# Weight conversion ordered behind head pairs, and three streamed operands moved to another place in SBUF

## The chip, the cores and the metric

One core of a Trainium2 chip runs the whole program. The metric is the device time of one execution in microseconds (us), and the median of several executions is compared. The engines are TensorE (PE, with its weight loads, PEld, shown apart), VectorE (DVE), ScalarE (ACT), GpSimd (POOL) and the DMA queue that SyncE (SP) issues.

## The reference, cut to what matters

```python
def phi(x):
    proj = x @ w_phi
    proj = proj - max(abs(proj), axis=-1)
    return concatenate([exp(proj), exp(-proj)], axis=-1)
q_p, k_p = phi(q), phi(k)                  # 8 batches x 8 heads, 576 x 64 -> 576 x 256
num = q_p @ (k_p.T @ v)
den = q_p @ sum(k_p, axis=sequence) + 1e-6
x   = num / den                            # heads side by side: 8 x 576 x 512
u   = x + (relu(x.T @ w_tok1) @ w_tok2).T  # 576 -> 256 -> 576
out = u + relu(u @ w_ch1) @ w_ch2          # 512 -> 1536 -> 512
```

Everything is float32. `w_ch1` and `w_ch2` are `wc1` and `wc2` in the kernel. They come from the host as 8-byte numbers.

## The kernel before, in words

Heads are worked in 32 pairs, four to a batch. Five generators emit the program, and `weave` (L547) decides by a virtual clock whose step comes next. Each generator yields the cost of its step, which is divided by its share: `keys` and `queries` 5.2, `token_stream` 8.0, `load_weights` 10.0, `channel_stream` 19.5. A generator that yields None waits in the emission for another one. The order so emitted is a priority: a scheduler then fixes each engine's own order by times that it models, and may let a later instruction whose operands are ready go first. On the chip each engine keeps the order that came out.

`keys` (L246) loads a pair, makes feature maps of the keys in five groups (`less_max`, L184: a product with the feature weights, the absolute maximum, a subtraction; then two exponentials, L265), and `add_kv` (L276) sums features times values in PSUM: `pkv`, L287, with `kp` stationary and the value tile `v` streamed. When the fifth group is in, ACT copies the sum to SBUF (`kv`, L298). `queries` (L304) does the same for queries, turns the feature rows with TensorE transposes (`pt`, L343, the identity `ident` streamed), takes exponentials and multiplies by `kv` (`pn`). Pairs 0 to 3 (`PLAIN`) are multiplied in plain float32, with `wp` streamed (L209) and `qf` streamed (L377). Later pairs are split into two float32r parts and take three products (`mm3`, L70) with `wp2`, `qh` and `ql` streamed. For pairs 0 to 7 (`EARLY`) the reciprocal of the denominator goes through DRAM in small DMAs on SP's queue (L391 to L399).

`token_mix` (L416) needs two attended pairs of a batch. It transposes with `ident` streamed (`px`, L423). `channel_mix` (L462) takes 256 tokens at a time through six up-projections (`h`, stationary `wc1_h` and `wc1_l`, streamed `uh` and `ul`) and six down-projections (`acc`, stationary `wc2`, streamed `gh` and `gl`), 24 matmuls of 256 columns each. An up-projection `ep` waits in the emission until `wc2` rows 2ep and 2ep+1 are converted (L504).

`load_weights` (L137) converts the weights from 8-byte numbers to two float32r parts. One `convert` (L107) is a DMA of 512 KB on SP (`rawc`, L118), an absolute value on ACT (L124), four bit operations on DVE (L125 to L128, tile `bitsc`), a rounding copy on ACT and a subtraction on POOL. After seven small conversions for `w1` and `w2` there are 24 large ones, in three groups of eight: four of 512 columns of `wc1` and four row blocks of `wc2`. Four staging buffers (`late0` to `late3`) are shared by them. `pace()` yields 8.0 before pair 3 is attended and 1.0 after.

SBUF pools lie one behind the other: `cst`, `wk`, `st`, `odd`. `cst` begins with a tile of 32 bytes, `st` with one of 192 bytes, and nearly every other tile of `cst`, `wk` and `st` is a multiple of 512 bytes. So stationary operands (in `cst` and `wk`) share one starting phase modulo 512 bytes, and the float32r streamed operands (in `st`) share one that lies 192 bytes further. `ident` and `wp` are in `cst`. The value tiles `v0` and `v1` are in `odd`, with 65 floats (260 bytes) from one slice to the next.

Of the kernel before, what the change touches and what calls it, by code (L numbers as in the profile page):

```python
# [8 lines left out]
F32 = mybir.dt.float32  # L9
# [3 lines left out]
AF = mybir.ActivationFunctionType  # L13
# [4 lines left out]
P = 128  # L18
B, H, S, D = 8, 8, 576, 64
NP = H // 2  # L20
F = 128
# [4 lines left out]
PLAIN = 4  # L26
EARLY = 8
BORROWED = 18
STAGES = 4
LAST = 15  # L30
LAG = 0.02
# [11 lines left out]
def mixer_kernel(ctx, tc, qk, vm, vt, w_phi, w1, w2, wc1, wc2d, out):  # L43
    nc = tc.nc

    cst = ctx.enter_context(tc.tile_pool(name="cst", bufs=1))
# [3 lines left out]
    st = ctx.enter_context(tc.tile_pool(name="st", bufs=2))  # L50
    odd = ctx.enter_context(tc.tile_pool(name="odd", bufs=2))
# [10 lines left out]
    def split(hi, lo, raw, eng_hi, eng_lo):  # L62

        if eng_hi is nc.scalar:
            nc.scalar.copy(hi, raw)
        else:
            eng_hi.tensor_copy(hi, raw)
        eng_lo.tensor_tensor(lo, raw, hi.bitcast(F32), op=ALU.subtract)
# [6 lines left out]
                             skip_group_check=group_ok)  # L75


    ident = cst.tile([P, P], F32, name="ident")
    make_identity(nc, ident)
    eps = odd.tile([P, 1], F32, tag="eps", name="eps", bufs=1)  # L80
    nc.gpsimd.memset(eps, 1e-6)
    wp2 = st.tile([P, 2, F], F32R, tag="wp2", name="wp2", bufs=1)
    wp = cst.tile([P, F], F32, name="wp")
    nc.scalar.dma_start(wp[D:], w_phi)
    nc.scalar.dma_start(wp[:D], w_phi)
    split(wp2[:, 0], wp2[:, 1], wp, nc.vector, nc.vector)
# [8 lines left out]

    vtiles = []
    for j in range(2):
        t = odd.tile([P, 5, 2, D + 1], F32, tag=f"v{j}", name=f"v{j}", bufs=1)
        nc.gpsimd.memset(t[:, 4], 0.0)
        nc.gpsimd.memset(t[:, 0:4, :, D:], 1.0)  # L100
        for i in range(2):
            nc.gpsimd.memset(t[i * D:(i + 1) * D, 4, i, D:], 1.0)
        vtiles.append(t)

    nstage = [0]

    def convert(hi, lo, srcs, name, tag=None):  # L107

        w, n = hi.shape
        if tag is None:  # L110
            tag = f"late{nstage[0] % STAGES}"
            nstage[0] += 1
        raw = wk.tile([P, 4, 256], U32, tag=tag, name=f"raw{name}", bufs=3 if tag == "xt1" else 1)
        raw = raw.rearrange("p a b -> p (a b)")[:w, :2 * n]
        at = 0
        for src in srcs:
            m = src.shape[1]
            nc.sync.dma_start(raw[:, 2 * at:2 * (at + m)].bitcast(I64), src)  # L118
            at += m
        raw = raw.rearrange("p (n two) -> p n two", two=2)  # L120
        top, low = raw[:, :, 1], raw[:, :, 0]
        m = wk.tile([P, 512], U32, tag="bits", name=f"bits{name}", bufs=3)[:w, :n]

        nc.scalar.activation(m.bitcast(F32), top.bitcast(F32), AF.Abs)  # L124
        nc.vector.tensor_scalar(m.bitcast(F32), m.bitcast(F32), LEAST, MOST, op0=ALU.max, op1=ALU.min)  # L125
        nc.vector.tensor_scalar(m, m, 3, 0x3FFFFFF8, op0=ALU.logical_shift_left, op1=ALU.bitwise_and)
        nc.vector.scalar_tensor_tensor(m, top, 0xC0000000, m, op0=ALU.bitwise_and, op1=ALU.bitwise_or)
        nc.vector.scalar_tensor_tensor(m, low, 29, m, op0=ALU.logical_shift_right, op1=ALU.bitwise_or)  # L128
        split(hi, lo, m.bitcast(F32), nc.scalar, nc.gpsimd)

    def flat(t):
        return t.rearrange("p a b -> p (a b)")

    def pace():
        return 1.0 if NP - 1 in attended else 8.0

    def load_weights():  # L137
        for u in (0, 3):
            s = UNITS[u][2]
            convert(flat(w1_h[:, u:u + 2]), flat(w1_l[:, u:u + 2]),  # L140
                    [w1[s + o:s + o + P] for o in (0, P)], f"1_{u}")
            yield 1.0
        convert(w1_h[:D, 2], w1_l[:D, 2], [w1[512:]], "1_2")
        for w in (w1_h, w1_l):
            nc.scalar.copy(w[D:, 2], w[:D, 2].bitcast(F32))
        yield 0.4
        for u in range(NT):
            rows = w2[u * P:(u + 1) * P]
            convert(w2_h[:, u, :256], w2_l[:, u, :256], [rows[:, :256]], f"2_{u}")
            yield 0.5  # L150
            convert(w2_h[:, u, 256:], w2_l[:, u, 256:], [rows[:, 512:], rows[:, 256:512]], f"3_{u}")
            yield 0.7
        for e in range(0, E, 512):
            for c in range(NC_):
                convert(wc1_h[:, c, e:e + 512], wc1_l[:, c, e:e + 512],
                        [wc1[c * P:(c + 1) * P, e:e + 512]], f"c1_{c}_{e}")
                yield pace()
            for k in range(e // P, e // P + 4):
                src = wc2d[k * P:(k + 1) * P]
                late = k - (NE - STAGES)  # L160
                if late < 0:
                    t, tag = cst.tile([P, 2, C], F32R, name=f"wc2_{k}"), None
                else:
                    t = wk.tile([P, 2, C], F32R, tag=f"late{late}", name=f"wc2_{k}", bufs=1)
                    tag = f"late{late + 1}" if late + 1 < STAGES else "xt1"
                wc2.append(t)
                convert(t[:, 0], t[:, 1], [src], f"c2_{k}", tag)
                loaded.add(k)
                yield pace()

# [13 lines left out]
    def less_max(ts, units, name, base=None):  # L184
# [4 lines left out]
        if base == D:  # L189
            ps = ps_a.tile([P, 2, 2, F], F32, tag=f"a{nplain['k'] % 2}", name=f"pp{name}")  # L190
            nplain["k"] += 1
        elif base == 0 and (nplain["q"] % 2 == 0 or nplain["q"] >= BORROWED):
            ps = ps_h.tile([P, 2, 2, F], F32, tag="h", name=f"pp{name}")
# [52 lines left out]
    def keys():  # L246
        groups = [[(0, 0), (0, 1)], [(0, 2), (0, 3)], [(1, 0), (1, 1)], [(1, 2), (1, 3)], [None]]
        todo = None
        for i in range(B * NP):
            yield from until(lambda: i < 2 or i - 2 in asked)  # L250
            if i < PLAIN:
                load_plain(i)
            else:
                load(i)
            v_sb, queue = vtiles[i % 2], nc.sync if i else nc.scalar
            queue.dma_start(v_sb[:, 0:4].rearrange("p u j d -> p (u j) d")[:, :, :D], vm[i])
            for j in range(2):
                queue.dma_start(v_sb[j * D:(j + 1) * D, 4, j, :D], vt[i, j])
            plain = D if i < PLAIN else None
            ts = pairs[i] if i < PLAIN else stack(raws[i], D, f"k{i}")  # L260
            for g, us in enumerate(groups):
                pm = less_max(ts, us, f"k{i}_{g}", plain)
                kp = wk.tile([P, 2, 2, F], F32, tag="kp", name=f"kp{i}_{g}")
                for sg in range(2):
                    nc.scalar.activation(kp[:, :len(us), sg], pm[:, :len(us)], AF.Exp, scale=1.0 - 2.0 * sg)  # L265
                yield 0.22
                if todo:
                    add_kv(*todo)
                    yield 0.82
                todo = (i, g, us, kp, v_sb)  # L270
        add_kv(*todo)
        yield 0.82
# [3 lines left out]
    def add_kv(i, g, us, kp, v_sb):  # L276
        if g == 0:
            pkvs[0] = ps_k.tile([P, 2, 2, D + 1], F32, tag="kv", name=f"pkv{i}")
        pkv = pkvs[0]
        for n, u in enumerate(us):  # L280
            for sg in range(2):
                if u is None:
                    o = pkv[:, sg].rearrange("p j d -> p (j d)")
                    v = v_sb[:, 4].rearrange("p j d -> p (j d)")
                else:
                    o, v = pkv[:, sg, u[0]], v_sb[:, u[1], u[0]]
                nc.tensor.matmul(o, kp[:, n, sg], v, start=g == 0 and n == 0 and sg == 0, stop=u is None,  # L287
                                 skip_group_check=True)
        if g < 4:
            return  # L290

        both = []
        for k in range(1 if i < PLAIN else 2):
            kv = wk.tile([P, 2, 4, D], F32 if i < PLAIN else F32R, tag=f"kv{k}", name=f"kv{k}_{i}", bufs=1)
            for at, src in ((slice(0, 4, 3), pkv[:, :, :, :D]),
                            (slice(1, 3), pkv[:, :, :, D:].to_broadcast([P, 2, 2, D]))):
                if k == 0:
                    nc.scalar.copy(kv[:, :, at], src)  # L298
                else:
                    nc.vector.tensor_tensor(kv[:, :, at], src, both[0][:, :, at].bitcast(F32), op=ALU.subtract)  # L300
            both.append(kv)
        kvs[i] = both
# [103 lines left out]
    def until(cond):  # L406
        while not cond():
            yield None
# [138 lines left out]
    def weave(streams):  # L547
# [3 lines left out]
        while streams:  # L551
# [13 lines left out]

    weave([(keys(), 5.2, True), (queries(), 5.2, True), (token_stream(), 8.0, False),
           (load_weights(), 10.0, False), (channel_stream(), 19.5, False)])


# [40 lines left out]
```

## Time and profile before

| | us |
|---|---|
| median of 3 executions | 1162.64 |
| range of the 3 | 1160.67 to 1170.23 |
| the profiled execution, device time | 1164.33 |
| its span, first to last instruction | 1162.2 |
| PE / PEld busy in the span | 1121.3 / 1090.5 |
| DVE / ACT / POOL busy in the span | 685.7 / 659.4 / 570.1 |

The profile is one execution. "Busy" counts the time in which an engine had an instruction in work. Matmuls overlap one another in the record, so the time from one matmul to the next is read from the chain of waits (a piece with its count), and not from the mean length of one. In the windows, "x" is the number of instructions that touch the stretch, and PEclk is the mean granted TensorE clock in it, 1.00 for 2.4 GHz and 0.50 for 1.2 GHz.

### The profile page before, as it was taken

To read this page: it belongs to the slowest core of one execution; us is meant where nothing else is said; L and a number is where in the kernel's file an instruction comes from. 1 tells how busy PE (TensorE), PEld (TensorE's weight loads), DVE (VectorE), ACT (ScalarE), POOL (GpSimd) and SP (SyncE) were. 2 spreads that over 40 slices of the span, in tenths; PEclk is the share of its full clock that TensorE was granted. 3 is DMA by queue.
4 is the path that set the end of the run, shared out by engine and by line. 5 is a ranking of instruction groups with operands and counts; after the bars stand their busy time and mean duration, and the time that the engine had idled before them with its cause. 6 is when DMAs were issued, how large, how long until landed. Compare 5 with 4: busy or idle time off the path is not lost.

```text
span 1162.2 us, 24135 instructions
## 1 busy us (share of the span) xinstructions
PE 1121.3 (96%) x9032; PEld 1090.5 (94%) x9032; DVE 685.7 (59%) x1446; ACT 659.4 (57%) x1845; POOL 570.1 (49%) x734
## 2 busy tenths in 40 slices
PE   8987799999999999999999999999999999999998
PEld 7766699998999899999999999999999989999998
DVE  7989763536656665667566465573666666553111
ACT  5678785666656665666657465563655666441110
POOL 3347773555545564566646354563554655430000
PEclk9988999999999999999999999999999999999999
DMA  8564130111111011111111011110111110000000
GB/s 224 162 187 135 42 88 24 47 43 54 32 28 52 21 41 41 32 49 32 32 49 33 19 32 50 32 50 13 38 48 33 50 31 11 20 1 19 19 19 19
DMA packets 72531, 56.77 MB, mean 49 GB/s; under 512 B 49920, under 2 KB 63648, under 8 KB 72416
## 3 DMA queue, kind: packets, MB, share of 16 engines
q1 hardware_dynamic: 71056, 54.89, 16.7%
q8 instruction: 71, 1.16, 0.4%
q10 hardware_dynamic: 1360, 0.36, 0.2%
q14 instruction: 44, 0.36, 0.1%
HBM read 45.72 MB, written 9.51 MB: 48 GB/s over the span
## 4 chain that ended last, share of the span: by engine, by line
PE 85%; ACT 5%; DVE 4%; DMA 3%; issue 1%; POOL 1%; SPq 0%; POOLq 0%; DVEq 0%; ACTq 0%
PE acc L74 25%; PE h L74 25%; PE pkv L287 9%; PE pn L74 7%; PE ph L74 4%; PE pa L74 3%; PE pt L343 3%; PE ppk L205 2%; PE ppq L205 2%; DMA inv<-few 1%; PE px L423 1%; PE pn L377 1%; PE ppk L209 1%; ACT qh L356 1%; ACT qf L350 1%
## 5 line engine op out<-in xcount | busy, mean ns | idle before, releaser
L74 PE MATMUL acc<-gh,wc 128*128 128x256 f32 x1728 | 336.5, 282 | 0.2 <-ACT gh L489 0.2
L74 PEld LDWEIGHTS acc<-gh,wc 128*128 128x128 f32 x1728 | 274.0, 189 | 0.5 <-ACT gh L489 0.4
L74 PE MATMUL h<-ul,wc_h 128*128 128x256 f32 x864 | 243.4, 282 | 1.9 <-POOL ul L470 1.8
L74 PE MATMUL h<-uh,wc_h 128*128 128x256 f32 x864 | 244.8, 284 | 0.5 <-DVE gl L490 0.5
L74 PE MATMUL h<-uh,wc_l 128*128 128x256 f32 x864 | 243.7, 282 | 0.0
L74 PE MATMUL acc<-gl,wc 128*128 128x256 f32 x864 | 242.3, 282 | 0.0
L287 PE MATMUL pkv<-v,kp 128*128 128x65 f32 (+1 forms) x1152 | 165.7, 280 | 0.4 <-ACT kp L265 0.3
L74 PEld LDWEIGHTS h<-ul,wc_h 128*128 128x128 f32 x864 | 163.1, 189 | 2.7 <-POOL ul L470 2.7
L74 PEld LDWEIGHTS h<-uh,wc_h 128*128 128x128 f32 x864 | 162.6, 188 | 1.2 <-DVE gl L490 1.1
L74 PEld LDWEIGHTS h<-uh,wc_l 128*128 128x128 f32 x864 | 163.4, 189 | 0.0
L74 PEld LDWEIGHTS acc<-gl,wc 128*128 128x128 f32 x864 | 162.8, 188 | 0.0
L287 PEld LDWEIGHTS pkv<-v,kp 128*128 128x128 f32 x1152 | 156.9, 203 | 4.0 <-issue 1.8
L265 ACT ACTIVATE kp<-pmk 128x256 f32<-128x256 f32 (+1 forms) x320 | 109.3, 392 | 89.0 <-POOL pmk L221 83.7
L357 POOL TENSOR_TENSOR ql<-qf,qh 128x320 fp32r<-128x320 f32 (+1 forms) x112 | 92.8, 828 | 135.9 <-ACT qh L356 133.2
L490 DVE SCALAR_TENSOR_TENSOR gl<-h,gh 128x512 fp32r<-128x512 f32 x108 | 74.0, 686 | 140.3 <-ACT gh L489 139.6
L350 ACT ACTIVATE qf<-pt 128x320 f32<-128x320 f32 (+1 forms) x256 | 105.2, 414 | 84.6 <-PE pt L343 83.9
L489 ACT ACTIVATE gh<-h 128x512 fp32r<-128x512 f32 x108 | 64.6, 598 | 102.5 <-PE h L74 101.8
L74 PE MATMUL pn<-qh,kv 128*128 128x320 f32 (+1 forms) x448 | 114.9, 297 | 1.7 <-DVE pq L214 0.8
L402 POOL TENSOR_TENSOR xt<-xt,den 128x320 f32<-128x320 f32 x64 | 53.8, 840 | 116.7 <-DVE den L401 36.6
L357 DVE TENSOR_TENSOR ql<-qf,qh 128x320 fp32r<-128x320 f32 (+1 forms) x112 | 71.1, 635 | 65.0 <-ACT qh L356 64.6
L221 POOL TENSOR_TENSOR pmk<-pk,mxk 128x256 f32<-128x256 f32 (+1 forms) x140 | 86.8, 620 | 30.0 <-DVE mxk L219 23.2
L180 POOL TENSOR_TENSOR stq<-raw,stq 64x512 fp32r<-64x512 f32 (+1 forms) x56 | 79.8, 1424 | 40.5 <-ACT stq L179 36.4
(109 smaller groups left out, 2420.8 us busy)
## 6 DMA issues: line engine op xcount, KB each, us to landing
raw<-in_qk SPq DMA_DIRECT2D x27, 576.0 KB, 4.0
rawc<-in_wc SPq DMA_DIRECT2D x24, 512.0 KB, 4.8
v<-in_vm SPq DMA_DIRECT2D x31, 256.0 KB, 3.9
out_x<-xt SPq DMA_DIRECT2D x12, 256.0 KB, 2.2
out_x<-xt SPq DMA_DIRECT2D x16, 192.0 KB, 2.0
raw<-in_w SPq DMA_DIRECT2D x8, 256.0 KB, 3.5
out_x<-xt SPq DMA_DIRECT2D x16, 128.0 KB, 3.0
pair<-in_qk SPq DMA_DIRECT2D x8, 160.0 KB, 3.8
```

The source lines that it names most:

```text
L74: nc.tensor.matmul(o, a, m, start=first and i == 0, stop=last and i == 2, skip_group_check=group_ok)
L180: nc.gpsimd.tensor_tensor(t[lo:lo + D], src, t[base:base + D].bitcast(F32), op=ALU.subtract)
L205: nc.tensor.matmul(ps[:, i].rearrange("p two f -> p (two f)"), t[:, c:c + P], wp2.rearrange("p two f -> p (two f)"), start=True, stop=True)
L221: eng.tensor_tensor(pm[:, :n], pr, mx[:, :n].unsqueeze(2).to_broadcast([P, n, F]), op=ALU.subtract)
L265: nc.scalar.activation(kp[:, :len(us), sg], pm[:, :len(us)], AF.Exp, scale=1.0 - 2.0 * sg)
L287: nc.tensor.matmul(o, kp[:, n, sg], v, start=g == 0 and n == 0 and sg == 0, stop=u is None, skip_group_check=True)
L343: nc.tensor.transpose(ptr[:, n], r, ident)
L350: nc.scalar.activation(full, src, AF.Exp, scale=1.0 - 2.0 * sg)
L357: (nc.gpsimd if sg else nc.vector).tensor_tensor(lo, full, hi.bitcast(F32), op=ALU.subtract)
L402: nc.gpsimd.tensor_tensor(x, x, den, op=ALU.mult)
L489: nc.scalar.activation(gh, ph, AF.Relu)
L490: nc.vector.scalar_tensor_tensor(gl, ph, 0.0, gh.bitcast(F32), op0=ALU.max, op1=ALU.subtract)
```

## The change

The 24 large conversions get a gate for each group of eight. In the emission, group 0, 1 and 2 wait until the `kv` copy of pair 2, 3 and 4 has been emitted, and the first ACT instruction of each conversion is put behind that copy in ACT's queue (`issue_after` adds an order on the same engine and no semaphore). The identity, the plain feature weights and the value tiles move into the pool `st`, the value slices with 128 floats (512 bytes) from one to the next, so that all of them begin at the phase of the other streamed operands. The two value tiles grow from 2,600 to 5,120 bytes a partition each. The product of the fifth key group writes and reads its two heads as a strided shape in place of a flat one.

```diff
+FROM = 2
...
-    ident = cst.tile([P, P], F32, name="ident")
+    ident = st.tile([P, P], F32, tag="ident", name="ident", bufs=1)
...
-    wp = cst.tile([P, F], F32, name="wp")
+    wp = st.tile([P, F], F32, tag="wp", name="wp", bufs=1)
...
-        t = odd.tile([P, 5, 2, D + 1], F32, tag=f"v{j}", name=f"v{j}", bufs=1)
+        t = st.tile([P, 5, 2, 128], F32, tag=f"v{j}", name=f"v{j}", bufs=1)[:, :, :, :D + 1]
...
-    def convert(hi, lo, srcs, name, tag=None):
+    summed = {}
+
+    def convert(hi, lo, srcs, name, tag=None, behind=None):
...
-        nc.scalar.activation(m.bitcast(F32), top.bitcast(F32), AF.Abs)
+        with tc.issue_after(summed[behind].ins) if behind is not None else nullcontext():
+            nc.scalar.activation(m.bitcast(F32), top.bitcast(F32), AF.Abs)
...
         for e in range(0, E, 512):
+            pair = FROM + e // 512
+            yield from until(lambda: pair in summed)
             for c in range(NC_):
                 convert(wc1_h[:, c, e:e + 512], wc1_l[:, c, e:e + 512],
-                        [wc1[c * P:(c + 1) * P, e:e + 512]], f"c1_{c}_{e}")
+                        [wc1[c * P:(c + 1) * P, e:e + 512]], f"c1_{c}_{e}", None, pair)
                 yield pace()
...
-                convert(t[:, 0], t[:, 1], [src], f"c2_{k}", tag)
+                convert(t[:, 0], t[:, 1], [src], f"c2_{k}", tag, pair)
...
-                    o = pkv[:, sg].rearrange("p j d -> p (j d)")
-                    v = v_sb[:, 4].rearrange("p j d -> p (j d)")
+                    o, v = pkv[:, sg], v_sb[:, 4]
...
-                    nc.scalar.copy(kv[:, :, at], src)
+                    summed[i] = nc.scalar.copy(kv[:, :, at], src)
```

## Rows read from the trace of the kernel before

**Rows 1.** The page: PE's busy time, then its tenths and granted clock in 40 slices.
```profile
PE 1121.3 (96%) x9032; PEld 1090.5 (94%) x9032; DVE 685.7 (59%) x1446; ACT 659.4 (57%) x1845; POOL 570.1 (49%) x734
...
PE   8987799999999999999999999999999999999998
...
PEclk9988999999999999999999999999999999999999
```

**Rows 2.** Windows: stretch, length, PE, PEld, DVE, ACT, POOL busy (count), PEclk, DMA share, GB/s.
```profile
27.00:58.00 31.00, 30.70 (x109) 24.47 (x107) 30.04 (x61) 21.01 (x49) 11.43 (x8) 1.00 0.58 172
58.00:73.00 15.00, 13.34 (x88) 10.41 (x87) 12.42 (x29) 13.14 (x34) 8.48 (x7) 1.00 0.68 205
73.00:100.00 27.00, 19.48 (x91) 15.74 (x92) 25.02 (x45) 18.56 (x45) 12.96 (x11) 0.81 0.63 164
100.00:130.00 30.00, 25.51 (x153) 21.61 (x152) 27.33 (x56) 24.60 (x64) 23.20 (x22) 0.89 0.34 97
130.00:160.00 30.00, 26.34 (x206) 24.75 (x205) 20.05 (x47) 25.00 (x70) 20.73 (x27) 1.00 0.21 59
...
150.00:200.00 50.00, 49.88 (x427) 49.48 (x426) 23.36 (x56) 33.66 (x95) 28.83 (x40) 1.00 0.15 43
```

**Rows 3.** Chain of waits, two pieces of one kind: start, length, what, count.
```profile
37.74 3.60 PE pkv L287 x16
...
63.17 1.73 PE pkv L287 x16
```

**Rows 4.** ACT in order of time: the kv copies of pairs 2, 3 and 4.
```profile
72.97 0.65 ACT L298 COPY kv<-pkv 128x256 f32<-128x256 f32 x2
...
100.62 0.64 ACT L298 COPY kv<-pkv 128x256 f32<-128x256 f32 x2
...
127.49 0.64 ACT L298 CAST kv<-pkv 128x256 fp32r<-128x256 f32 x2
```

**Rows 5.** Windows, instructions on bitsc alone: DVE, ACT, POOL busy (count), PEclk, DMA.
```profile
27.00:58.00 31.00, 22.96 (x33) 9.80 (x16) 9.42 (x6) 1.00 0.58 172
58.00:73.00 15.00, 7.73 (x13) 4.00 (x7) 5.68 (x4) 1.00 0.68 205
73.00:100.00 27.00, 20.88 (x27) 8.93 (x14) 8.99 (x7) 0.81 0.63 164
100.00:130.00 30.00, 17.95 (x21) 6.21 (x10) 8.05 (x6) 0.89 0.34 97
```

**Rows 6.** Chain of waits between 80 and 110 us, three of its pieces.
```profile
80.49 6.51 DMA inv<-few
...
100.13 1.79 DMA inv<-few
...
109.37 1.42 DVE bitsc L128
```

**Rows 7.** Chain of waits, pieces of matmuls after the start of the channel mix.
```profile
155.02 2.83 PE h L74 x24
...
163.85 0.79 PE h L74 x7
...
182.58 2.13 PE h L74 x18
...
303.11 1.59 PE h L74 x14
...
306.97 0.22 PE pt L343 x2
...
307.30 0.59 PE acc L74 x5
...
1050.38 0.57 PE pa L74 x5
...
1053.67 0.61 ACT ah L448
...
1152.59 5.67 PE acc L74 x48
```

## The prediction

> **What bounds the kernel now.** I read the page first, then windows over the first 200 us, then the chain of waits, and last the rows of the weight conversion. The page shows PE busy for 96% of the span, and the slices place nearly all that is missing in the first five of forty, some 145 us [rows 1]. From 150 us on PE has no room: 49.88 of 50 us busy, while DVE is at 23.36 [rows 2]. So a change can gain only in two ways: less time lost before about 155 us, or a faster pace of the matmuls after it. The two halves of the change aim at one each.
>
> The start has two parts. Up to 58 us PE is busy without a break (30.70 of 31 us), though DVE is nearly full beside it (30.04) [rows 2]. The pace there is low: sixteen products of features and values take 3.60 us at 37.74 and 1.73 us at 63.17 [rows 3]. The window's 1.00 can't be right for that stretch: the pace is half, which fits the lower level of 1.2 GHz and then 2.4 GHz. From 58 to 160 us PE is idle for 1.66, 7.52, 4.49 and 3.66 us of the four stretches, 17.3 us in all, and the granted clock averages 0.81 and 0.89 in the middle two [rows 2]. There DVE is the fuller engine (25.02 of 27, 27.33 of 30), and the chain runs through conversion work on DVE and the small transfers of the denominators [rows 2, 6].
>
> **The conversions, step by step.** A large conversion is four DVE instructions. Before 73 us 33 + 13 of them were touched, so 46/4 = 11.5 conversions, and pair 2's copy, behind which the first group now stands, comes at 72.97 [rows 4, 5]. Those 11.5 must be done later.
>
> (a) 27 to 58 us: 22.96 us of DVE, 9.80 of ACT and 9.42 of POOL leave [rows 5]. PE loses nothing there today, so I cost this at 0. The bound on the gain is PE's 0.30 us of idle; a loss has no source, since PE's work there doesn't change. Its cover is gone, though: DVE time that was free beside a slow PE is given up.
>
> (b) 58 to 73 us: 7.73 us of DVE leave [rows 5]. PE's idle 1.66 us there can go, and pairs 2 and 3 reach their copies sooner. What follows is the stretch with the lower clock: at a mean of 0.81 over 27 us the lower level held for 27 x 0.19 x 2 = 10.3 us; at PE's busy share there (19.48/27 = 0.72) half of 7.4 us is lost, 3.7 us. Bounds of (b): 0 to -5.4 us, and +3.7 if the lower level comes once more. I take -4, as pair 2's chain loses most of its bit operations.
>
> (c) From 73 us on: 11.5 more conversions. One costs 4 x 20.88/27 = 3.1 us of DVE at 73 to 100 and 4 x 17.95/21 = 3.4 us at 100 to 130, against 4 x 22.96/33 = 2.8 us in the early stretch [rows 5]: where POOL is busier the same four instructions take longer. So 11.5 x 3.2 = 37 us of DVE enter. The room is 87 - 72.40 = 14.6 us up to 160 [rows 2]; 22 us are left over. They need not be done by then. The first up-projection that reads the third group of `wc1` is the fifth, whose piece starts at 182.58 [rows 7], and the third group may start after pair 4's copy, now at 127.49 [rows 4]. From 150 to 200 us DVE has 26.6 us of room [rows 2], so the rest fits if DVE takes conversions behind the attention's work. No semaphore is added: the absolute values are only ordered behind the copy on ACT, so nothing on ACT waits longer than the copy. Queued behind a late conversion are: on ACT its rounding copy and then the exponentials of the next keys, on POOL its subtraction and then those of the features, and on SP its 512 KB load (24 in all, one each) ahead of the loads of `raw` and `v` and the denominators' small transfers. One of these took 6.51 us where another took 1.79 [rows 6]; one more such delay is 4.7 us, on the chain only until pair 3 is attended. Bounds of (c): 0, and +22 if the 22 us of DVE all end on the path. I take +2, near the lower end, because of the due times.
>
> **The operands' phase.** After 155 us the chain shows two paces of the same 256-column float32r matmuls. Slow: 24 in 2.83 us, 117.9 ns each, the first at 155.02 and the last at 1152.59. Fast: 14 in 1.59 us, 113.6 ns, the first such piece at 163.85 and the last at 1050.38 [rows 7]. Counted one by one between these rows, 3,458 go at the slow pace and 2,398 at the fast, so the slow pace costs 3,458 x 4.3 = 14.9 us. A pair of transposes that stream the identity (306.97) is followed by the slow pace (5 in 0.59 us, 118 ns), and so after nearly all of them. But a wait alone does the same: PE waits for ACT at 1053.67, nothing that the change moves runs after that, and the slow pace holds to the end [rows 7]. That last stretch holds about 104 us / 2.83 x 24 = 880 matmuls, 3.8 us of the 14.9, which the change can't reach. Of the other 11.1 us I take a third, -4, since the identity is followed by the slow pace but isn't its only cause. Bounds: -11.1 us, and +10.3 us if the fast 2,398 all turn slow. The sixteen value products of 63.17 read four slices of different phase (260 bytes a step) and run on as one unbroken piece [rows 3], so I cost `v`'s own move at 0 within 2 us either way (16 in 1.73 us are 108 ns, against 113.6 ns of the fast pace). Plain `wp` is used in the first pairs alone, 72 products, and costs 0. The strided fifth group does the same work: 0.
>
> A rule speaks against this half. The Trainium skill, TensorE: Matmul & The Clock Gate, section "What happens when you issue a matmul", says that PE has two independent read ports of SBUF, so that loading the next weights takes nothing from the running matmul. By it the place of an operand is worth 0 and the sum would be -2. The two paces of rows 7 show that something makes the same work slower, but no row shows that it is the place.
>
> **The sum.** 0 - 4 + 2 - 4 = -6 us against the profiled execution's 1164.33 us (span 1162.2 and 2.1 around it): 1158.3. That execution is 1.7 us above the median of the runs shown, so the median should come to 1156.6, rounded 1157.
>
> **The rivals.** Each is given against the median of 1162.64.
>
> Phase is the lever. The moved identity lets the fast pace go on wherever the program, not a wait, ended it: all 11.1 us, with the ramp at -2. 1162.6 - 13.1 = 1149.5. For it: the slow pace behind the transposes. Against it: the slow pace behind a wait.
>
> The ramp clears. Pairs 2 and 3 run without bit operations in their way, and of PE's 17.3 us idle between 58 and 160 us two thirds go, with the 3.7 us of lower clock: 1162.6 - 11.5 - 3.7 - 4 = 1143.4. For it: conversion work in the chain [rows 6]. Against it: all 24 conversions still stand in that stretch or just behind it.
>
> The conversions crowd. The place is DVE between pair 2's copy and the first channel block. If its order puts each group as a burst right behind its copy, ahead of the next pair's work, the 22 us that don't fit before 160 us land on the path. PE then keeps part of its work in that time; between 22 x 0.18 (its idle share, 15.7 of 87 us) = 4 and 22 I take 13, with no gain from the phase: 1162.6 + 13 = 1175.6. It decides as soon as more than 14.6 us of bit operations are done before batch 0's token mix is over. For it: the early DVE time that is given up was free. Against it: the due times.
>
> Nothing. The order of conversions is hidden anyway, and the place of an operand does nothing: -2 at most, 1160.6. This is what the page named above would give, as a mechanism of this kernel: weight reads and streamed reads don't meet.
>
> **How the numbers follow.** Chances: forecast 0.31, phase 0.25, ramp 0.14, crowding 0.19, nothing 0.11. A measurement of this kernel can tell about 1% from no change, 11.6 us, so faster means below 1151.0 and slower above 1174.3. Faster: over half of phase (0.14), nearly all of ramp (0.13) and a sixth of the forecast's spread (0.05), 0.32. Slower: most of crowding (0.16) and 0.02 of the forecast, 0.18. The rest, 0.50, is within 1%. The range reaches from the centre of the ramp case, 1143, to just under that of crowding, 1174; about 0.07 is left out below and 0.11 above. The forecast's own range is 1149 to 1166.
>
> **What would show it.** (a) right: up to 58 us PE is still unbroken and the value products still go at about 3.6 us for sixteen, with DVE far below 30 of 31 us. (b) right: the copies of pairs 2 and 3 come some us before 72.97 and 100.62. (c) right: conversions run to about 180 us, and the second up-projection of the first channel block starts no later than 155.02; wrong if it starts at 165 or later, or if PE waits for a converted weight. The phase: pieces behind a pair of identity transposes go on at 113.6 ns, and the slow count falls from 3,458 to about 2,500; wrong if 118 ns still stands behind them. The whole forecast is wrong if the time before the second up-projection moves by more than 10 us, or if the pace from 160 us to the end moves by more than 1%.

## The result, and the profile after

| | before | after |
|---|---|---|
| median of 16 executions each, us | 1166.76 | 1175.33 |
| their range, us | 1160.67 to 1175.48 | 1171.04 to 1181.39 |
| the profiled execution, device time (span), us | 1164.33 (1162.2) | 1181.39 (1179.5) |

The ratio of after to before is 1.0076, with a 95% interval of 1.005 to 1.0102. The kernel is slower, by 8.6 us on the medians. That is less than the 1% that the prediction called distinguishable, but these 32 executions do set it apart from no change. More executions also moved the median of before from 1162.64 to 1166.76 us: the three that were shown lay low. The profiled execution of after is the longest of its sixteen, so the two traces differ by 17.1 us where the medians differ by 8.6. What follows reads the place and the kind of the loss from these two traces and takes the size of an effect from the medians.

First the page of after, in answer to [rows 1]: busy time, then tenths and granted clock in 40 slices.

```profile
PE 1124.0 (95%) x9032; PEld 1095.4 (93%) x9032; DVE 696.4 (59%) x1446; ACT 660.0 (56%) x1845; POOL 575.6 (49%) x734
...
PE   7986789998999999999999999999999999999998
...
DVE  6569994445746666566656466574665666553111
...
PEclk9978689999999999999999999999999999999999
```

The gaps of PE and of its clock still lie in the first slices, up to some 180 us. DVE has moved: slices 4 to 6, 90 to 175 us, are full. DVE's sum has grown by 10.7 us with the same 1,446 instructions.

The windows of after, in answer to [rows 2], with the same columns:

```profile
27.00:58.00 31.00, 29.83 (x195) 24.55 (x192) 17.16 (x51) 20.83 (x60) 5.10 (x6) 1.00 0.43 124
58.00:73.00 15.00, 13.23 (x52) 10.19 (x50) 8.41 (x21) 10.37 (x26) 4.26 (x3) 0.67 0.31 89
73.00:100.00 27.00, 21.34 (x102) 17.76 (x102) 23.28 (x41) 20.20 (x51) 15.99 (x14) 0.75 0.46 127
100.00:130.00 30.00, 21.53 (x134) 19.30 (x132) 29.90 (x54) 22.99 (x57) 25.12 (x23) 0.87 0.55 161
130.00:160.00 30.00, 21.16 (x100) 18.96 (x100) 29.87 (x49) 20.97 (x54) 23.09 (x21) 0.69 0.44 131
150.00:200.00 50.00, 43.42 (x314) 42.01 (x313) 39.38 (x71) 32.32 (x84) 33.60 (x34) 0.88 0.25 73
200.00:250.00 50.00, 49.91 (x422) 49.36 (x421) 22.18 (x53) 30.40 (x88) 23.79 (x34) 1.00 0.14 38
```

And the same stretches for the instructions on `bitsc` alone (DVE, ACT, POOL, clock, DMA), in answer to [rows 5]; the two last stretches have no row there, and before had 2.21 us on DVE in the first of them and none in the second.

```profile
27.00:58.00 31.00, 0.00 (x0) 0.00 (x0) 0.00 (x0) 1.00 0.43 124
58.00:73.00 15.00, 6.10 (x11) 2.42 (x4) 1.76 (x1) 0.67 0.31 89
73.00:100.00 27.00, 17.16 (x19) 6.95 (x11) 6.71 (x5) 0.75 0.46 127
100.00:130.00 30.00, 22.08 (x26) 8.87 (x14) 11.21 (x7) 0.87 0.55 161
130.00:160.00 30.00, 22.17 (x23) 6.35 (x10) 7.37 (x5) 0.69 0.44 131
160.00:200.00 40.00, 16.79 (x18) 5.62 (x9) 8.40 (x6) 0.89 0.19 52
```

Two things are to be seen. From 27 to 58 us PE works on 195 instructions where it had 109, in nearly the same busy time: the conversions are gone, the granted clock is at its upper level from 32.4 us on, and the attention runs ahead. From 100 to 160 us DVE is busy for 59.8 of 60 us, PE for 42.7 (51.9 before), and the clock averages 0.69 in the second half where it was 1.00. From 200 us on PE is full again (49.91 of 50 us).

The early lead is real, and it is lost again. The kv copies of pairs 2 to 6 in after (ACT in order of time), beside [rows 4]:

```profile
61.42 0.64 ACT L302 COPY kv<-pkv 128x256 f32<-128x256 f32 x2
...
84.18 0.65 ACT L302 COPY kv<-pkv 128x256 f32<-128x256 f32 x2
...
114.47 0.63 ACT L302 CAST kv<-pkv 128x256 fp32r<-128x256 f32 x2
...
155.67 0.64 ACT L302 CAST kv<-pkv 128x256 fp32r<-128x256 f32 x2
...
199.77 0.65 ACT L302 CAST kv<-pkv 128x256 fp32r<-128x256 f32 x2 [1.94 <-PE pn L75]
```

Against [rows 4] pairs 2, 3 and 4 are 11.6, 16.4 and 13.0 us earlier. Pairs 5 and 6, which came at 154.95 and 180.99 before, are 0.7 and 18.8 us later. From one copy to the next it took 22.8 us, and then 30.3, 41.2 and 44.1. Pair 0's copy, ahead of every large conversion, is already 2.5 us later in this execution (26.60 against 24.08).

The chain of waits of after shows what stands there: pieces between 137 and 144 us, then the end.

```profile
138.57 1.64 DVE bitsc L130
140.21 1.41 DVE bitsc L128
141.62 1.95 DVE bitsc L131
...
143.59 0.62 ACT wc L66
...
179.52 3.64 PE h L75 x17
...
1169.88 5.67 PE acc L75 x48
```

Three bit operations follow one another on the chain, 5.0 us together, where [rows 6] had a single one of 1.42 us. What PE wants of DVE stands behind them in DVE's order (one row of DVE and one of PE in order of time; the bracket is PE's idle time and what ended it):

```profile
144.54 0.42 DVE L219 TENSOR_TENSOR pq<-ppq,partq 128x256 f32<-128x256 f32 x1
...
145.10 0.55 PE L75 MATMUL pn<-qh,kv 128*128 128x256 f32 x1 [3.16 <-DVE pq L219]
```

From 73 us to the second up-projection PE waits for 23.7 us, and 22.4 us of it end with a DVE instruction (some 17 and 15 us in before). The 17 matmuls at 179.52 take 214 ns each: the granted clock there is 0.5, 1.2 GHz, after a stretch (172.0 to 179.2 us) in which PE was busy for 5.01 of 7.20 us. The second up-projection of the first channel block starts at 168.46 us, where it started at 154.77 (PE in order of time). The last down-projection starts 17.3 us later than in [rows 7]. Most of the loss, 13.7 of these 17.3 us, is there before the channel mix has got going, the 2.5 us of pair 0's late copy among it.

**DVE's account** can be drawn up from the windows of both traces. Idle time given up between 27 and 73 us: 20.4 us in after less 3.5 in before, 16.9. Bit operations dearer: 84.3 us in all against 71.7, 12.6. Idle time taken up again between 73 and 160 us: 14.6 in before less 4.0 in after, 10.6. That leaves 16.9 + 12.6 - 10.6 = 18.9 us of DVE work to be done after 160 us, and the window there does have 16.8 us of bit operations that before did not have.

Why they are dearer shows in one of the four, the clamp (min/median/max ns, first and last start), first in before:

```profile
L125 DVE TENSOR_SCALAR bitsc<-bitsc x24: 408/426/1496, 28.2 to 155.1; 128x512 f32<-128x512 f32 x24
```

and in after:

```profile
L128 DVE TENSOR_SCALAR bitsc<-bitsc x24: 408/790/1504, 62.9 to 175.2; 128x512 f32<-128x512 f32 x24
```

The shortest and the longest are as before, but the median has nearly doubled. POOL is busy for 5.10 of 31 us in the stretch that the conversions left and for 48.2 of 60 us where they went. The Trainium skill, SBUF — State Buffer, section "Who interferes with whom", says that DVE in some of its modes and GpSimd lock one another out of a port pair for a whole instruction. These rows agree with that in direction; no run here isolates the lock.

### The profile page after: what moved, and what is told of

The parts are those of the page before. It is cut to its first block, busy times and chain, and to the rows that moved or that the text cites. A ratio compares the mean times of both kernels' runs of the same rounds, so it can differ in the third digit from the quotient of the medians.

```text
span 1179.5 us, 24131 instructions
## 1 busy us (share of the span) xinstructions
PE 1124.0 (95%) x9032; PEld 1095.4 (93%) x9032; DVE 696.4 (59%) x1446; ACT 660.0 (56%) x1845; POOL 575.6 (49%) x734
## 4 chain that ended last, share of the span: by engine, by line
PE 83%; DVE 6%; ACT 5%; DMA 3%; issue 2%; POOL 1%; SPq 0%; POOLq 0%; DVEq 0%; ACTq 0%
PE acc L75 25%; PE h L75 24%; PE pkv L291 9%; PE pn L75 7%; PE ph L75 3%; PE pa L75 3%; PE pt L347 3%; PE ppk L210 2%; PE ppq L210 2%; DVE bitsc L130 1%; PE pn L381 1%; PE px L427 1%; DVE bitsc L131 1%; PE ppq L214 1%; DVE bitsc L128 1%
## 5 line engine op out<-in xcount | busy, mean ns | idle before, releaser
L75 PE MATMUL pn<-qh,kv 128*128 128x320 f32 (+1 forms) x448 | 116.0, 300 | 4.0 <-DVE pq L219 3.2
L185 POOL TENSOR_TENSOR stk<-raw,stk 64x512 fp32r<-64x512 f32 (+1 forms) x56 | 81.4, 1453 | 40.0 <-ACT stk L184 28.6
```

The costliest lines, as they stand in the source:

```text
L75: nc.tensor.matmul(o, a, m, start=first and i == 0, stop=last and i == 2, skip_group_check=group_ok)
L185: nc.gpsimd.tensor_tensor(t[lo:lo + D], src, t[base:base + D].bitcast(F32), op=ALU.subtract)
```

## The experiments

Ratios are to the kernel before on the same chip, with a 95% interval. "Gates" are the two edits to the conversions (the wait in the emission and `issue_after`). "Places" are the moves of identity, feature weights and values together with the strided fifth group.

**Which half costs.** One kernel has the gates alone, one the places alone, and the second was run twice, on two chips.

```diff
 e1_gate_only: the change without these; ident, wp, v and the flat fifth group as before
-    ident = st.tile([P, P], F32, tag="ident", name="ident", bufs=1)
-    wp = st.tile([P, F], F32, tag="wp", name="wp", bufs=1)
-        t = st.tile([P, 5, 2, 128], F32, tag=f"v{j}", name=f"v{j}", bufs=1)[:, :, :, :D + 1]
 e2_phase_only, f1_phase_only_again: the change without these
-            yield from until(lambda: pair in summed)
-        with tc.issue_after(summed[behind].ins) if behind is not None else nullcontext():
```

> The gates alone, identity, feature weights and values left at their old places; every engine's order of instructions is that of the changed kernel. Crowding theory (the whole loss is bit operations of the conversions pushed together on DVE between 100 and 180 us): the same ratio to the kernel before as the whole change had, 1.0076, between 1.004 and 1.012, DVE over 29 of 30 us busy at 100 to 130 and at 130 to 160, the second up-projection of the first channel block near 168 us. Rival, the moved operands are what costs: 1.000 within 0.003.

> The moved identity, feature weights and values alone, no gates; every engine's order is that of the kernel before. Crowding theory: 1.000 within 0.003, pieces behind a pair of identity transposes still at 118 ns. Rival, the moved operands cost: 1.004 to 1.012. Rival, they help and the gates lose more than the sum shows: 0.990 to 0.996, with 113.6 ns behind the transposes.

> The moved operands alone, a second time. If moving them gives something: 0.995 to 0.998 again and an interval that leaves out 1. If the first 0.9969 was the spread of the runs: 1.000 within 0.003, and the slow pace behind the transposes as before.

Measured: the gates alone 1177.17 us, ratio 1.0082 (1.0048 to 1.0117). The places alone 1162.28 us, 0.9969 (0.9942 to 0.9997), and again 1168.01 us, 0.9992 (0.9956 to 1.0027). So the gates carry the whole loss, and the gain of the first places run did not come again. The gates-alone trace has the order of after on every engine, and its windows show the same picture:

```profile
27.00:58.00 31.00, 28.73 (x197) 23.09 (x195) 15.75 (x49) 22.12 (x62) 5.25 (x5) 1.00 0.34 100
...
100.00:130.00 30.00, 23.00 (x113) 20.60 (x113) 29.87 (x54) 19.16 (x48) 25.30 (x24) 0.72 0.47 142
130.00:160.00 30.00, 22.50 (x116) 21.10 (x115) 29.86 (x49) 20.65 (x55) 21.14 (x20) 0.65 0.46 142
```

This execution took 1170.23 us, the shortest of its seven, and its second up-projection starts at 159.96 us, not near 168 as expected: 5.2 us later than in before, with pair 0's copy at 24.08 in both. So after's 13.7 us is the upper end, and the 8.6 us of the medians lies between the two.

The places-alone traces, which have the order of before on every engine, answer a question on before that its own trace could not: what bounds 27 to 58 us. First its window in the first run of the two, then that of 58 to 73 us in the second:

```profile
27.00:58.00 31.00, 25.66 (x108) 19.81 (x107) 30.38 (x62) 20.80 (x49) 12.19 (x9) 0.72 0.60 178
```

```profile
58.00:73.00 15.00, 15.00 (x57) 11.87 (x57) 6.57 (x16) 7.52 (x20) 3.80 (x3) 0.50 0.51 166
```

In the first the clock was at its upper level for ten of the 31 us (30.7 to 40.9), and PE idled for 5.3 us. Yet it worked on 108 instructions where before, busy for 30.70 us, had 109, and the copies of pairs 1 and 2 came at 53.16 and 73.04 us against 53.55 and 72.97. A faster PE gained nothing, and DVE was busy for 30.38 us. DVE sets the pace there, and PE's full row in before was a slow clock stretching its work over DVE's time. In the second run the lower level held from 39 to 80 us, PE became the bound at 58 to 73 us, and the second up-projection started at 162.6 us in place of 154.8. That is 8 us from one execution to another with no instruction in another place of the order, about half of the spread of before's sixteen executions.

**Which part of the gates.** The wait in the emission kept and `issue_after` taken away (once with the old places, once with the new), and the groups gated behind earlier or later pairs.

```diff
 e4_gate_emission_only (old places), f2_emission_moved (new places)
-        with tc.issue_after(summed[behind].ins) if behind is not None else nullcontext():
-            nc.scalar.activation(m.bitcast(F32), top.bitcast(F32), AF.Abs)
+        nc.scalar.activation(m.bitcast(F32), top.bitcast(F32), AF.Abs)
 e7_gate_from0 (old places)
-FROM = 2
+FROM = 0
 f3_gate_from3 (old places)
-FROM = 2
+FROM = 3
```

> The gates in the emission alone, without the order on ACT behind the copy, old places. The scheduler may then draw conversions forward into the early holes of DVE again. Crowding theory: conversions start before 50 us, fewer of them fall after 100 us, and the time lies between before and the changed kernel, 1.000 to 1.005. Rival, the loss comes from the later emission and not from where conversions run: 1.0076 again.

> The gates in the emission alone together with the moved operands: the change without the order on ACT. If both small gains are real and add up: 0.990 to 0.995. If the moved operands do nothing: that of the emission gates alone, 0.993 to 0.999.

> The gates alone, but behind pairs 0, 1 and 2 in place of 2, 3 and 4. Crowding theory: conversions start near 27 us again and end well before 170, the loss is mostly gone, 0.996 to 1.003. Rival, a gate as such costs: 1.006 or more.

> The gates alone, with the order on ACT, behind pairs 3, 4 and 5. Crowding theory (DVE time given up early and wanted back at 100 to 180 us): a larger loss than behind pairs 2 to 4, 1.012 to 1.025, second up-projection of the first channel block at 170 us or later. Rival, the loss is a fixed cost of an order on ACT: 1.005 to 1.010 again.

Measured: without `issue_after` 1162.29 us, 0.9959 (0.9929 to 0.9988), with the old places, and 1168.64 us, 0.9995 (0.9965 to 1.0026), with the new. The two kernels have the same order on every engine, their intervals overlap, and no gain is certain. But the loss is gone in both. Neither ratio lies in a range that was expected: the first is below 1.000 to 1.005, the second above 0.993 to 0.999. With the old places, DVE spends 22.61 us on bit operations between 27 and 58 us, as before did (22.96): the scheduler draws them forward whatever the emission says. So the wait in the emission is harmless, and the order on ACT is what holds the conversions back.

Behind pairs 0, 1 and 2 the ratio is 0.9994 (0.9957 to 1.0031), with 22.39 us of bit operations in that stretch. Behind 2, 3 and 4 it is the 1.0082 above, and behind 3, 4 and 5 1.0107 (1.0047 to 1.0168). The last was expected at 1.012 or more; its point lies below that, though the intervals leave room, and the last two ratios aren't told apart. Behind pairs 0, 1 and 2 the same order on ACT holds nothing back: the first clamp starts at 29.3 us. Behind 3, 4 and 5 the loss moves back with the groups. The windows behind 3, 4 and 5:

```profile
130.00:160.00 30.00, 19.87 (x120) 18.83 (x120) 29.61 (x50) 17.76 (x46) 21.37 (x21) 0.77 0.53 159
150.00:200.00 50.00, 41.66 (x291) 40.16 (x291) 47.74 (x74) 31.34 (x76) 35.38 (x34) 0.85 0.30 81
```

DVE is nearly full up to 200 us (47.74 of 50 from 150 us on), and the second block's first up-projection comes 12 us later than in before (215.9 against 203.6). The first block's second, expected at 170 us or later, starts at 152.5 and isn't late at all.

**Is it DVE's time?** In two kernels two of the four bit operations of every conversion are left out: the clamp, and the merging in of the low word's top bits. So the weights there lack both. A third kernel moves the clamp to POOL.

```diff
 e5_before_half_bits (of before), e6_gate_half_bits (of the gates alone)
-        nc.vector.tensor_scalar(m.bitcast(F32), m.bitcast(F32), LEAST, MOST, op0=ALU.max, op1=ALU.min)
...
-        nc.vector.scalar_tensor_tensor(m, low, 29, m, op0=ALU.logical_shift_right, op1=ALU.bitwise_or)
 f4_emission_clamp_pool (of the emission wait alone, old places)
-        nc.vector.tensor_scalar(m.bitcast(F32), m.bitcast(F32), LEAST, MOST, op0=ALU.max, op1=ALU.min)
+        nc.gpsimd.tensor_scalar(m.bitcast(F32), m.bitcast(F32), LEAST, MOST, op0=ALU.max, op1=ALU.min)
```

> The kernel before with two of the four bit operations of every conversion left out (the clamp and the merge of the low word), some 36 us of DVE in the first 160 us. If DVE bounds the first 150 us: 0.980 to 0.992 of before, with DVE no longer near full at 27 to 58. If PE's low clock bounds it up to 58 us, as the prediction had it: 0.993 to 1.000, the copy of pair 1 still near 53 us.

> The gates alone, with the same two bit operations left out. Crowding theory: the gates' loss goes away with the DVE work that is crowded, so this lies within 0.4% of the ungated kernel with half the bit operations, or below it, where the full ones had 0.8% between them. Rival, the gates lose by the order on the other engines (ACT, SP, PE): still 0.6 to 1.0% above it.

> The emission gates alone, and the clamp of every conversion on POOL in place of DVE. If DVE's work bounds the first 160 us and POOL has room: 0.985 to 0.995, some 15 us of DVE less before 160 us. If POOL's longer instruction stands in the chain of each conversion, or holds DVE up: 0.997 to 1.01.

Measured: before with half the bit operations 1158.63 us, 0.9867 (0.9776 to 0.9958); the gates with half 1157.36 us, 0.9895 (0.984 to 0.9951). Less work on DVE makes the kernel faster by some 1%, so DVE is a bound of the start. It is not the only one: with half the work DVE is busy for 22.96 of 31 us at 27 to 58, and pair 1's copy still comes at 52.63 us, the sign named for PE's low clock (no upper level is on record there before 42.5 us). And the gates, which cost 0.8% with the whole work, leave 0.3% with half of it, and their median is the lower one. No loss can be told there, but the two intervals are wide enough for one of 0.8%. That fits a price paid in DVE time without proving it; DVE's full rows and PE's waits for it show it more directly.

The clamp on POOL is a miss as a remedy: 1175.08 us, 1.0068 (1.0038 to 1.0099). Its row, and the window where it shows:

```profile
L127 POOL TENSOR_SCALAR bitsc<-bitsc x24: 1910/1920/2358, 35.4 to 171.4; 128x512 f32<-128x512 f32 x24
```

```profile
100.00:130.00 30.00, 19.74 (x110) 17.03 (x111) 22.36 (x40) 18.05 (x48) 29.68 (x25) 0.77 0.47 128
```

The clamp takes 1.92 us on POOL where DVE's median was 0.43, and POOL fills up (29.68 of 30) in DVE's place.

**Does the distance between operands matter at all?** The moved operands did nothing, so the distance of all streamed float32r operands from the stationary ones was changed, by the size of the first tile of `st`. All of `st` and the pool behind it move along; nothing else changes, and every engine keeps the order of before.

```diff
-    st.tile([P, 48], F32, tag="lead", name="lead2", bufs=1)
+    st.tile([P, 128], F32, tag="lead", name="lead2", bufs=1)
```

This is the first; the others have 16, 32, 40, 56 and 64 floats in place of 48.

> The kernel before with 512 in place of 192 bytes ahead of the streamed operands, so that streamed and stationary operands begin at the same phase; order unchanged. If the place of the streamed operands sets the two paces: over 0.5% slower or faster than before, another share of 118 ns. If place is nothing: 1.000 within 0.003 and both paces as before.

> The kernel before with 256 bytes ahead of the streamed operands in place of 192, half the repeat of 512; order unchanged. If the distance of streamed and stationary operands modulo 512 sets the share of the fast pace (none of it fast at a distance of 0): another share than the 2,398 of 5,856 of before, in either direction, and a time that follows it by 4.4 ns a matmul. If only equal phase is special: the share of before within 500 matmuls and 1.000 within 0.004.

> The kernel before with 64 bytes ahead of the streamed operands in place of 192; order unchanged. Distances of 0 and 256 bytes leave no fast pace. If the pattern repeats every 128 bytes, 64 gives the share of 192, near 40% fast, and 1.000; if it repeats every 256, another share than 192, its time following by 4 to 6 ns a matmul.

> 128 bytes ahead of the streamed operands. If the pattern repeats every 128 bytes: no fast pace, 1.018. If it repeats every 256: a share of its own, and if the distance as such is what counts, the largest one, up to all fast, 0.985 to 0.995.

> 160 bytes ahead of the streamed operands. If the fast share grows smoothly with the distance from 0 and 256: more fast than at 192, 0.990 to 0.998. If only whole steps of 64 bytes count: no fast pace or that of 128.

> 224 bytes ahead of the streamed operands. If the fast share grows with the distance from 256: less fast than at 192, 1.005 to 1.015. If it doesn't: within 0.4% of before.

The last column is counted from each trace behind 160 us: the mean time from one 256-column matmul's start to that of the next one right behind it, steps of 130 ns and more (transposes or waits) left out.

| distance, bytes mod 512 | ratio | interval | mean step, ns |
|---|---|---|---|
| 0 (e3) | 1.0172 | 1.0136 to 1.0207 | 119.7 |
| 64 (e9) | 1.0057 | 1.0013 to 1.01 | 117.2 |
| 128 (e10) | 1.0133 | 1.0055 to 1.0211 | 118.9 |
| 160 (e11) | 1.0113 | 1.0031 to 1.0195 | 118.4 |
| 192 (before) | 1 | | 116.0 |
| 224 (e12) | 1.011 | 1.0046 to 1.0174 | 118.3 |
| 256 (e8) | 1.0185 | 1.0121 to 1.025 | 119.7 |

The mean step and the ratio go together: some 5,750 such steps, 3.7 ns longer at a distance of 0, are 21 us, 1.8% of the kernel. Between the traces of the other kernels at 192 bytes it varies from 115.5 to 116.2 ns.

The chain of waits at a distance of 0, in the channel mix:

```profile
1102.10 2.88 PE h L74 x24
1104.98 2.88 PE acc L74 x24
```

24 matmuls take 2.88 us, 120.0 ns each, where the slow pace of [rows 7] is 117.9, and the fast pace of 113.6 hardly occurs: 36 of 5,746 steps are below 116 ns, where before has 2,361 of 5,742. The second up-projection starts when it did in before (154.80 against 154.77 us) and the end comes 21.6 us later, so all of it is pace. At 256 it is the same. So the place of the streamed operands does set the pace of these matmuls, and of the seven tried the kernel before already has the best. No run moves the stationary operands, so their distance and the streamed operands' own address can't be told apart. The expectations named simple patterns, and these fail: 64 isn't like 192, so nothing repeats every 128 bytes, and 160 and 224 are both slower than 192, so the fast pace doesn't grow with the distance from 0 and 256.

The same instructions in the same order go at 120.0 ns or at 113.6 ns with nothing changed but the place. So what the prediction drew from the rule that it named (the Trainium skill, TensorE: Matmul & The Clock Gate, "What happens when you issue a matmul": two independent read ports), that the place of an operand is worth 0, does not hold for the streamed float32r operands as a whole. Whether the weight loads have a part in it no run shows, so the rule itself is neither confirmed nor refuted. For the three operands that the change moves its outcome was the right one.

## Why the prediction was wrong

The forecast was a small gain, 1157.0 us; the outcome is a small loss, 1175.33 us, above the range's top of 1174. Some 4 us of the distance come from the base, which three executions put too low. By ratio the forecast was -0.5% and the result is +0.8%.

**(a) failed**: "PE loses nothing there today, so I cost this at 0" and "a loss has no source, since PE's work there doesn't change". The step read PE's full row as the bound. The first places-alone run shows that it was not. After does show DVE far below 30 of 31 us, as the step's sign said, but not the pace: PE works on 86 more instructions in the stretch, and sixteen value products take 1.73 us at 47.86 (chain of waits), not 3.6. The text did see that DVE time "is given up", but gave that no price at this step; it is 16.9 us in the account above. The conversions were not free there either: they held the attention up. With them gone and the clock up, pairs 2 to 4 come 12 to 16 us sooner, and that had no term; no run has the conversions gone with the clock still down.

**(b) had the right sign and was too small.** Pairs 2 and 3 came sooner by 11.6 and 16.4 us, where the term was 4. But no part of it reaches the end, since pairs 5 and 6 give it back. PE's idle time from 58 to 160 us, which was to shrink, grew from 17.3 to 24.7 us.

**(c) was mis-sized, and this decided the sign.** I took +2, "near the lower end, because of the due times". By the step's own sign (wrong at 165 us or later) it failed: the second up-projection starts at 168.46 us, 13.7 us late, and at 159.96, 5.2 us late, in the gates-alone trace; the medians are 8.6 us apart. Two things were wrong. First, the due times were kept well enough (the fifth up-projection, which needs the third group, starts at 196.2 us, and the last bit operation at 181.7), but they do not matter: DVE does its work in a fixed order, and the conversions stand in it before the work of pairs 5 and 6 and of the token mix for which PE waits. The runs without `issue_after` (no loss) and those with other pairs (0.9994 behind pair 0 on, 1.0082 and 1.0107 behind pairs 2 and 3 on) show that the cause is the hard order, where it holds the conversions back. Second, 3.2 us of DVE a conversion was taken from stretches in which POOL was in part less busy; it became 84.3/24 = 3.5 us over all 24, against 71.7/24 = 3.0. The step had seen that they are dearer beside POOL, but counted only the 11.5 that move.

**The operands' phase** was given -4 and is worth 0 within the resolution (0.9969, then 0.9992). The sign named for it failed: behind a pair of identity transposes the first step between two 256-column matmuls is slow (116 ns or more) in 93 of 93 cases in after and in 92 of 92 in before, though in 9 and 10 of them the pace is back at 113 ns a few matmuls later. Of the steps counted for the table above, 3,647 are at 116 ns or more in after and 3,381 in before; other executions with the streamed operands 192 bytes off have, for instance, 2,799 (gates alone) and 3,706 (places alone, second run). The count varies from execution to execution, and does not follow the moved operands. The 72 products of plain `wp` that the prediction counted are the keys' alone; there are 144 with the queries', and their move shows no cost either.

**The rivals.** What happened is the crowding case, with 0.19: its mechanism, its place (DVE between pair 2's copy and the first channel block) and its point of decision. Bit operations between 73 and 160 us grew by 61.4 - 41.0 = 20.4 us, above its 14.6. Its price of +13 lies between the medians (+8.6) and the two traces (+17). What spoke for it, the early DVE time that is given up, stood in [rows 5], and the due times were allowed to outweigh it. The gates themselves do what they say: the first clamp of a large conversion starts at 62.9 us, behind pair 2's copy, in place of 28.2.

**Open.** Why the place of the streamed operands sets the pace, whether it is their distance from the stationary ones, and why 192 is better than 160 or 224. Whether the emission wait with the old places gains some tenths of a per cent (0.9959) or just fell well: a version that surely beats before was not found. What share of the dearer bit operations is due to POOL was not isolated. A gate that spares early DVE time and yet leaves DVE's order free between pairs 2 and 5 was not tried.

## What to carry to other kernels

When two engines are both full in a stretch, ask which would still be full if the other were faster; a PE at its lower clock fills whatever time another engine gives it, and a second execution with another clock can tell. Work that is moved later must find idle time on its own engine at the place where it lands, in that engine's fixed order; that it is due much later is no help when it stands in front of work that is due now. Say "later" by a priority that the scheduler may overrule, since a hard order takes from it the idle time that it had found.

## What was not expected of the hardware

The place in SBUF of the streamed operands, here given as their distance from the stationary ones, changes the pace of float32r matmuls of 256 columns: 113.6 or 117.9 ns at 192 bytes, 120.0 ns at 0 and at 256, 1.7 to 1.9% of this kernel. The granted clock in the first 100 us varies between executions of one order: in the places-alone runs it was up from 30.7 to 40.9 us and again from 58 us in one and down from 39 to 80 us in the other, and the second up-projection came 6.6 us apart (156.06 and 162.63). And the granted clock of 1.00 that is printed for before up to 58 us is no record (its first stands at 58.3): the value products ran at half pace there [rows 3].
